# Where two loads of a written instruction order stand: in the middle of the opening, or behind its end

## The chip, the cores and the metric

One core of one Trainium2 chip runs the whole program. The metric is the device time of one execution in microseconds (us). Within 0.2% (2 us here) two versions of this kernel are called the same.

## The reference, cut to what matters

Rotary attention, then a mixture of experts, then a dense block, one after the other, float32 throughout:

```python
q, k, v: (4, 8, 576, 64)                      # 4 batches, 8 heads, 576 tokens
q_rot, k_rot = rotate(q), rotate(k)           # rotary embedding
scores = q_rot @ k_rot.T / sqrt(64)
attn = exp(scores - max); attn /= attn.sum() + 1e-9
x = (attn @ v) -> (2304, 512)                 # heads side by side
expert = argmax(x @ w_gate)                   # 8 experts, one per token
x = gate_w * (relu(x @ w1[expert]) @ w2[expert])
out = relu(x @ w_in)**2 @ w_out
```

## The kernel before, in words

The attention goes through 16 pairs of heads (P = 0 to 15). For each pair the work is cut into small steps, each named by a token: a letter, the pair, and a part. The ones that matter here:

- `L5` loads q and k of pair 5 (a tile `qk` of 1,280 KB, one DMA, line 244). `V5` loads v of pair 5 (tile `V`, 320 KB, line 248).
- `Q5..0` to `Q5..2` apply the rotary embedding on GpSimd in place in `qk` (lines 460 and 456). `H5` rounds the result to a high part on ScalarE (`XH`, line 261), `W5` takes the rest as a low part on GpSimd (`XL`, line 269).
- `Z5` stacks high and low parts by ten DMAs inside the chip (line 286), five for each head of the pair: `kZ` twice, `qZ` from `XH`, `QH`, and `qZ` from `XL` (160 KB each, `QH` 128).
- `S5.2` is one 128-row block of scores on TensorE (lines 310 and 312, tile `ps`); it reads `kZ`, `qZ` and `QH`. `M` takes its maximum on VectorE (line 320), `X` its exponential on ScalarE (line 327). The first block of a pair to run is number 2.
- `U` and `O` turn the exponentials on TensorE (line 345, tile `pp`) and copy them out (`eT`, `eL`). `A5.0` and `A5.1` multiply by `V` (line 372, tile `av`), `G` copies the result to `X` (line 375), `J` projects it, `F` divides by the sums; after pair 3 the routing of the first batch of tokens begins (tiles `rt_...`, on VectorE and GpSimd).

The order is written out by hand. `at(t, f)` puts a step on a heap with a planned time. The 298 tokens of the list `ORDER` get equal shares of the time 0 to `UNTIL` (90.30). Every other step gets the time 15.954 P plus a number from `OFF`. Steps are then given out in the order of these times, and each engine, SyncE (SP) with its DMA queue too, works through its own instructions in that order. Planned times are only a sort key; they are not times of the profile.

Buffers are in rings of a few: `qk` has two, `V` has two, `kZ` and `qZ` have four. A load into a buffer waits, on SP, until the last reader of what was there before is done; what follows on SP waits behind it. The reader counts wherever it stands in the order, also behind the load: `L7` is given out ahead of `W5`, whose tile it overwrites, and waits for it.

All loads and all stacking DMAs of the attention are issued by SP, in one queue.

Of the kernel before, what the change touches and what calls it, by code (L numbers as in the profile page):

```python
# [59 lines left out]
def shape_constants():  # L60
# [27 lines left out]
    for b in range(B):  # L88
        for c in range(4):
# [17 lines left out]
OFF = dict(pair=15.954, load=-26.0, v=8.0, rope=-11.279, hi=0.235, lo=1.675, z=4.815,  # L107
           S=[21.118, 20.135, 15.671, 27.85, 18.735, 24.184, 28.378, 24.712, 17.071],
           max=[21.846, 20.96, 16.399, 28.578, 19.463, 24.912, 29.183, 25.517, 18.084],
           exp=[22.666, 21.951, 17.479, 29.363, 20.248, 25.697, 30.078, 26.412, 18.869],  # L110
           un=[32.589, 32.153, 35.217, 38.036, 36.617, 23.748, 28.906, 37.6, 35.653, 34.253, 33.817],
           out=[33.418, 34.148, 36.917, 39.025, 37.411, 29.788, 32.958, 38.405, 36.294, 35.538, 34.643],
           av=[41.194, 44.969], x=[46.747, 47.789], pj=54.426, fin=58.03)
UNTIL = 90.30
# [15 lines left out]
def attention(tc, rope, ident, qk, v, w_gate, xd, on_batch, later, ahead):  # L130
# [18 lines left out]
    def at(t, f):  # L149
        heapq.heappush(sched, (round(t, 3), len(T["n"]), f))  # L150
        T["n"].append(0)
# [39 lines left out]
    def warm(n):  # L191
        nc.tensor.matmul(T["warm"][:, 0:n], T["hi", 0][:, 0, 0:128], T["hi", 0][:, 0, 0:n], start=True, stop=True)

    def do(token):
        k, a = token[0], [int(i) if i else None for i in token[1:].split(".")] if token[1:] else []
        if k in "SMXAG":
            dict(S=scores, M=smax, X=sexp, A=values, G=gathered)[k](*a)
        elif k in "UO":
            (turn if k == "U" else turned)(a[0], UNITS[a[1]])
        elif k in "RQ":  # L200
            rotate(a[0], a[1], nc.vector if k == "R" else nc.gpsimd, a[2])
        elif k in "Ww":
            low(a[0], a[1] if a[1:] else None, None if k == "W" else nc.vector)
        elif k == "E":
            for i in range(a[0]):
                warm(288)
        elif k in "bcd":
            dict(b=lambda: rotate(0, 1, nc.vector, cols=Z), c=lambda: direct_high(0, Z), d=lambda: direct_low(0, nc.vector, Z))[k]()
        else:
            dict(H=high, Z=stack_up, L=load, V=load_v, J=project, F=finish, K=gate_weights)[k](*a)  # L210

    def direct_high(P, cols):


        x, h = T["qk", P], T["hi", P]
        to = min(cols.stop, 512)
        for j in range(2):
            r = slice(64 * j, 64 * j + 64)
            nc.scalar.activation(QH[P][j][r, cols.start:to], x[r, 0, 1, cols.start:to], AF.Copy)
        if cols.stop > 512:  # L220
            nc.scalar.activation(h[:, 1, 512:640], x[:, 0, 1, 512:640], AF.Copy)

    def direct_low(P, eng, cols):
        x = T["qk", P]
        to = min(cols.stop, 512)
        for j in range(2):
            r = slice(64 * j, 64 * j + 64)
            minus(eng, T["qZ", 2 * P + j][r, cols.start:to], x[r, 0, 1, cols.start:to], QH[P][j][r, cols.start:to].bitcast(F32))
        if cols.stop > 512:
            minus(eng, T["lo", P][:, 1, 512:640], x[:, 0, 1, 512:640], T["hi", P][:, 1, 512:640].bitcast(F32))  # L230
# [19 lines left out]
    def rotate(P, n, eng, step=None, cols=slice(0, 640)):  # L250
        x, a = T["qk", P], slice(0, 2) if n is None else slice(n, n + 1)
        for i, (f, o, y) in enumerate(((times, 0, TB[:, 0, a, cols]), (times, 1, TB[:, 1, a, cols]), (plus, 0, x[:, 1, a, cols]))):
            if step in (None, i):
                f(eng, x[:, o, a, cols], x[:, o, a, cols], y)
# [8 lines left out]
    def low(P, n=None, eng=None):  # L263
        if ("lo", P) not in T:
            T["lo", P] = zp.tile([128, 2, 640], F32R, name="XL", tag="XL", bufs=2)
        a = slice(0, 2) if n is None else slice(n, n + 1)
        args = T["lo", P][:, a], T["qk", P][:, 0, a], T["hi", P][:, a].bitcast(F32)
        if eng is None:
            nc.gpsimd.tensor_sub(*args)
        else:  # L270
            minus(eng, *args)
# [139 lines left out]
    def route(P, t=None):  # L411
        t = OFF["pair"] * P + OFF["fin"] + .02 if t is None else t
        d = next(T["route", P], None)
        if d is not None:
            t += d
            at(t, lambda: route(P, t))
# [4 lines left out]
    for P in range(NPAIR):  # L421
        def on(o, token):
            if token not in ORDER:
                at(OFF["pair"] * P + o, lambda: do(token))

        if P > 2:
            on(OFF["load"], f"L{P}")
            for i in range(3):
                on(OFF["rope"] + 2.93 * i, f"Q{P}..{i}")
            for k, o in (("H", "hi"), ("W", "lo"), ("Z", "z")):  # L430
                on(OFF[o], f"{k}{P}")
        if P > 0:
            on(OFF["v"] + (1.8 if P == NPAIR - 1 else 0), f"V{P}")
        for k, o in (("S", "S"), ("M", "max"), ("X", "exp"), ("U", "un"), ("O", "out"), ("A", "av"), ("G", "x")):
            for u, t in enumerate(OFF[o]):
                on(t, f"{k}{P}.{u}")
        on(OFF["pj"], f"J{P}")
        on(OFF["fin"], f"F{P}")
        if P % 4 == 3 and P + 1 < NPAIR:
            at(OFF["pair"] * P + OFF["fin"] + .02, lambda P=P: route(P))  # L440
# [848 lines left out]
```

## Time and profile before

| | |
|---|---|
| median of 3 runs | 985.91 us (985.28 to 986.06) |
| the profiled execution | 987.28 us |
| its span, first to last instruction | 985.5 us |
| TensorE busy (PE) | 962.2 us, 98% of the span |
| VectorE (DVE), ScalarE (ACT), GpSimd (POOL) busy | 535.9, 422.8, 321.9 us |
| mean granted TensorE clock | 0.993 of full speed |
| attention, from the first instruction to the last `av` | about 300 us |

The profile lists instructions with the us from the span's start. In a timeline a row is the start, the time from the first start to the last end of the merged instructions, the engine, the line, the operation and its tiles, how many, and in brackets the idle time of the engine before the row and what ended it. `SPq` is SP issuing a DMA; a row of it ends when the issue is done, not when the data has landed.

### The profile page before, as it was taken

Reading aid. Unit: us, or ns where it says so; the run is one execution under the profiler, and the core shown is the slowest. Engines: PE = TensorE matmul, PEld = TensorE weight load, DVE = VectorE, ACT = ScalarE, POOL = GpSimd, SP = SyncE. Lnnn points to the kernel's source line nnn. Section 1 sums busy time; section 2 is a strip of 40 time slices with the busy share of each in tenths; the row PEclk is TensorE's granted clock in tenths of the full one; section 3 lists DMA queues with packets and bytes.
Section 4 is the critical chain, followed back from the end, with each engine's and each line's share of the span. In section 5 each row is a group of like instructions: output and inputs, shape, how many; then the busy total and the mean of one; then the engine's idle time right before and its main releaser. Section 6 shows DMA issues by size and latency. Waiting matters only on the chain. (4 is left out here: it accounts for less than half of the span.)

```text
span 985.5 us, 15576 instructions
## 1 busy us (share of the span) xinstructions
PE 962.2 (98%) x5589; PEld 826.9 (84%) x5589; DVE 535.9 (54%) x949; ACT 422.8 (43%) x840; POOL 321.9 (33%) x261
## 2 busy tenths in 40 slices
PE   8997999999999999999999999999999999999997
PEld 8785787878787888888888789999999999999996
DVE  7775677777876345575586469522322323222222
ACT  4665566666552123352465358522322222222222
POOL 2886487888475222233254300010010100100101
PEclk9999899999999999999999999999999999999999
DMA  6884786877542834455486523100000200100000
GB/s 219 242 249 128 200 227 185 231 206 196 169 121 92 274 124 130 130 172 183 138 283 223 183 96 135 33 33 1 32 33 1 65 1 22 43 1 1 33 1 33
DMA packets 46353, 119.83 MB, mean 122 GB/s; under 512 B 8240, under 2 KB 9776, under 8 KB 43952
## 3 DMA queue, kind: packets, MB, share of 16 engines
q1 hardware_dynamic: 40752, 101.58, 33.7%
q0 software_dynamic: 4960, 16.43, 4.9%
q8 instruction: 46, 0.75, 0.3%
q10 hardware_dynamic: 544, 0.66, 0.2%
q14 instruction: 51, 0.42, 0.1%
HBM read 79.93 MB, written 15.11 MB: 96 GB/s over the span
## 5 line engine op out<-in xcount | busy, mean ns | idle before, releaser
L1115 PE MATMUL o<-Wo,gs 128*128 128x512 f32 x864 | 214.7, 393 | 0.0
L1094 PE MATMUL h<-xs,Wi 128*128 128x384 f32 x1008 | 189.6, 336 | 0.0
L1115 PEld LDWEIGHTS o<-Wo,gs 128*128 128x128 f32 x864 | 159.9, 188 | 28.6 <-DVE gs L1105 0.3
L1094 PEld LDWEIGHTS h<-xs,Wi 128*128 128x128 f32 x1008 | 178.2, 188 | 6.6
L1103 DVE SCALAR_TENSOR_TENSOR g<-h,r 128x384 f32<-128x384 f32 x80 | 44.6, 558 | 190.5 <-ACT r L1099 190.5
L327 ACT ACTIVATE e<-ps,mx 128x576 f32<-128x576 f32 x144 | 106.3, 740 | 90.2 <-DVE mx L320 90.0
L1130 POOL DMA_INDIRECT out_dram<-os,at x18 | 17.8, 989 | 369.3 <-DVE os L1125 309.9
L320 DVE TENSOR_REDUCE mx<-ps 128x1 f32<-128x576 f32 x144 | 105.7, 752 | 57.6 <-PE ps L312 57.1
L1099 ACT ACTIVATE r<-h 128x384 f32<-128x384 f32 x96 | 47.1, 491 | 204.7 <-PE h L1094 204.7
L917 PE MATMUL p_y<-W,hh 128*128 128x512 f32 x504 | 124.5, 403 | 0.8 <-ACTq L929 0.8
L888 PE MATMUL p_h<-W,xs 128*128 128x512 f32 x480 | 114.8, 394 | 0.0
L917 PEld LDWEIGHTS p_y<-W,hh 128*128 128x128 f32 x504 | 94.3, 191 | 22.6 <-ACTq L929 1.1
L888 PEld LDWEIGHTS p_h<-W,xs 128*128 128x128 f32 x480 | 88.5, 188 | 18.4 <-DVEq L929 0.7
L345 PE MATMUL pp<-ident,e 128*128 128x128 f32 x640 | 86.2, 275 | 1.6 <-DVE eT L361 1.3
L1105 DVE TENSOR_TENSOR gs<-g,gs 128x384 fp32r<-128x384 f32 x96 | 53.7, 559 | 56.1 <-ACT gs L1104 56.1
L310 PE MATMUL ps<-kZ,qZ 128*128 128x288 f32 x300 | 72.0, 330 | 8.7 <-DMA qZ<-XL 7.4
L460 POOL TENSOR_TENSOR qk<-qk,TB 128x1280 f32<-128x1280 f32 (+1 forms) x28 | 79.2, 2844 | 2.1 <-DMA qk<-in_qk_dram 2.1
L345 PEld LDWEIGHTS pp<-ident,e 128*128 128x128 f32 x640 | 74.6, 142 | 5.3 <-issue 2.6
L1104 ACT ACTIVATE gs<-g 128x384 fp32r<-128x384 f32 x96 | 50.4, 526 | 50.5 <-DVE g L1103 50.0
L372 PE MATMUL av<-eT,V 128*64 128x288 f32 x512 | 69.1, 412 | 0.0
L361 DVE COPY eT<-pp 128x512 f32<-128x512 f32 x96 | 64.2, 683 | 7.3 <-PE pp L345 6.0
L310 PEld LDWEIGHTS ps<-kZ,qZ 128*128 128x128 f32 x300 | 45.9, 192 | 20.7 <-issue 11.8
(237 smaller groups left out, 1208.0 us busy)
## 6 DMA issues: line engine op xcount, KB each, us to landing
qk<-in_qk_dram SPq DMA_DIRECT2D x14, 1280.0 KB, 6.4
raw<-in_moe_w_dram SPq DMA_DIRECT2D x30, 512.0 KB, 4.6
kZ<-XH SPq DMA_DIRECT2D x60, 160.0 KB, 2.9
rawa<-in_moe_w_dram SPq DMA_DIRECT2D x18, 512.0 KB, 3.6
w<-in_moe_w_in_dram SPq DMA_DIRECT2D x8, 1024.0 KB, 5.2
w<-in_moe_w_out_dram SPq DMA_DIRECT2D x8, 1024.0 KB, 5.4
V<-in_v_dram SPq DMA_DIRECT2D x16, 320.0 KB, 4.1
qZ<-XH SPq DMA_DIRECT2D x30, 160.0 KB, 2.9
```

What stands on the lines that cost most here:

```text
L310: nc.tensor.matmul(t[:, u, 0:288], Q1[:, qs], K1[:, k0 + 288 * u:k0 + 288 * u + 288], start=i == 0, stop=False)
L320: nc.vector.tensor_reduce(small("mx", P, 9)[:, s:s + 1], T["S", P, s][:, :, 0:288], axis=AX.XY, op=ALU.max, negate=True)
L327: nc.scalar.activation(ed.rearrange("p (u n) -> p u n", u=2), T["S", P, s][:, :, 0:288], AF.Exp, bias=T["mx", P][:, s:s + 1], accum_out=SS ...
L345: nc.tensor.transpose(t[:, c * 128:c * 128 + 128], src, ident)
L361: nc.vector.tensor_copy(o, i)
L372: nc.tensor.matmul(t[64 * j:64 * j + 64], V[:, j, kc], eT[:, j, kc, cs] if kc < 4 else eL[:, cs], start=kc == 0, stop=kc == 4)
L460: v.tensor_tensor(out=out, in0=a, in1=b, op=ALU.mult)
L888: nc.tensor.matmul(t[u], s[:, a, k], W1[:, b, k, 512 * u:512 * u + 512], start=n == 0, stop=n == 11)
L917: nc.tensor.matmul(t, s[:, a, k], W2[:, b, k], start=n == 0, stop=n == 23)
L1094: nc.tensor.matmul(t, W[:, a, k, fs], s[:, c, k], start=n == 0, stop=n == 11)
L1105: nc.vector.tensor_sub(gs[:, 1], g, gs[:, 0].bitcast(F32))
L1115: nc.tensor.matmul(self.T["o", b][c], gs[:, a, 128 * c:128 * c + 128], W[:, w], start=(f == 0 and n == 0), stop=(f == 15 and n == 2))
```

## The change

Steps that are not in `ORDER` get a planned time of at least `UNTIL`.

```diff
     for P in range(NPAIR):
         def on(o, token):
             if token not in ORDER:
-                at(OFF["pair"] * P + o, lambda: do(token))
+                at(max(UNTIL, OFF["pair"] * P + o), lambda: do(token))
```

Of all steps outside `ORDER` two have a planned time below 90.30: `L7` with 15.954 x 7 - 26.0 = 85.68, and `V5` with 15.954 x 5 + 8.0 = 87.77. All other steps keep their place. Both now have the time 90.30, behind the last token of `ORDER` (`Z5`, 90.00) and ahead of the next step (`Q6..2`, 90.305); `V5` comes first, since pair 5 is listed ahead of pair 7. The order around the place, with the moved steps in capitals marked by stars:

```
before  ... O3.0 U3.9 *L7* S4.5 S4.7 O3.9 M4.5 M4.7 A3.0 X4.5 *V5* V4 Q6..0 W5 Q6..1 F2 X4.7 U4.5 Z5 Q6..2 S4.3 S4.6 ... A3.1 ...
after   ... O3.0 U3.9 S4.5 S4.7 O3.9 M4.5 M4.7 A3.0 X4.5 V4 Q6..0 W5 Q6..1 F2 X4.7 U4.5 Z5 *V5* *L7* Q6..2 S4.3 S4.6 ... A3.1 ...
```

On SP's queue this reads, before: `L6 L7 V5 V4 Z5 Z6 L8 V6`; after: `L6 V4 Z5 V5 L7 Z6 L8 V6`. The other queues hold the same instructions in the same order.

## Rows read from the trace of the kernel before

**Rows 1.** The page, part 1: busy us, share of the span, instructions of each engine.

```profile
PE 962.2 (98%) x5589; PEld 826.9 (84%) x5589; DVE 535.9 (54%) x949; ACT 422.8 (43%) x840; POOL 321.9 (33%) x261
```

**Rows 2.** Waits of PE, whole span: us in total, times, longest; the two longest.

```profile
PE ps L310 <- DMA qZ<-XL: 7.4, 1, 7.4
PE warm L480 <- POOL ss L168: 1.5, 1, 1.5
```

**Rows 3.** Timeline of PE: start, us, line, operation, count, idle before it.

```profile
76.03 0.66 PE L372 MATMUL av<-eL,V 128*64 128x288 f32 x4
...
92.21 0.66 PE L372 MATMUL av<-eL,V 128*64 128x288 f32 x4
100.27 0.82 PE L310 MATMUL ps<-kZ,qZ 128*128 128x288 f32 x2 [7.41 <-DMA qZ<-XL]
...
104.40 1.04 PE L345 MATMUL pp<-ident,e 128*128 128x128 f32 x8
...
118.53 0.53 PE L310 MATMUL ps<-kZ,qZ 128*128 128x288 f32 x2
...
120.83 1.04 PE L345 MATMUL pp<-ident,e 128*128 128x128 f32 x8
...
135.78 0.53 PE L310 MATMUL ps<-kZ,qZ 128*128 128x288 f32 x2
```

**Rows 4.** Windows: stretch, us, busy of each engine, granted clock, DMA share, GB/s.

```profile
92.80:100.20 7.40, 0.06 (x2) 0.00 (x0) 0.00 (x0) 1.59 (x2) 5.62 (x2) 0.81 0.82 199
100.20:104.40 4.20, 4.13 (x19) 4.14 (x20) 1.79 (x4) 1.32 (x3) 2.94 (x2) 0.52 0.95 225
```

**Rows 5.** Timeline of SP's queue around the place.

```profile
81.69 0.33 SPq L244 DMA_DIRECT2D qk<-in_qk_dram  x1
82.11 11.12 SPq L248 DMA_DIRECT2D V<-in_v_dram  x2
93.28 1.12 SPq L286 DMA_DIRECT2D kZ<-XH  x2
```

**Rows 6.** Waits of SP's queue from 60 to 93.3 us: total, times, longest.

```profile
SPq L248 <- PE av L372: 14.0, 2, 10.3
SPq L244 <- POOL XL L269: 11.1, 1, 11.1
```

**Rows 7.** Timelines of ACT and POOL, 77 to 104 us.

```profile
77.13 1.28 ACT L261 ACTIVATE XH<-qk 128x1280 fp32r<-128x1280 f32 x1
...
78.71 2.95 POOL L269 TENSOR_TENSOR XL<-qk,XH 128x1280 fp32r<-128x1280 f32 x1
...
94.58 2.88 POOL L269 TENSOR_TENSOR XL<-qk,XH 128x1280 fp32r<-128x1280 f32 x1 [7.04 <-ACT XH L261]
97.41 5.73 POOL L460 TENSOR_TENSOR qk<-qk,TB 128x1280 f32<-128x1280 f32 x2
```

**Rows 8.** Issue to landing, whole span, by tile: `qZ`, then `qk`, then `V`.

```profile
DMA to landing us min/median/max: 2.7/3.1/4.3
DMA to landing us min/median/max: 4.8/6.1/7.2
DMA to landing us min/median/max: 3.7/4.1/7.0
```

**Rows 9.** DMA of 93 to 101 us: packets, MB, mean rate (stacking DMAs and one `V`).

```profile
DMA packets 797, 1.64 MB, mean 205 GB/s; under 512 B 141, under 2 KB 141, under 8 KB 797
```

**Rows 10.** Timelines of POOL, DVE and SP, 115 to 126 us.

```profile
115.98 0.26 POOL L452 TENSOR_TENSOR rt_d<-lg,rt_mx 128x40 f32<-128x40 f32 x1 [12.83 <-DVE rt_mx L529]
...
116.97 2.93 POOL L456 TENSOR_TENSOR qk<-qk 128x1280 f32<-128x1280 f32 x1
...
117.74 0.18 DVE L540 TENSOR_REDUCE rt_mn<-rt_im 128x5 f32<-128x40 f32 x1
119.36 0.76 DVE L320 TENSOR_REDUCE mx<-ps 128x1 f32<-128x576 f32 x1 [1.44 <-PE ps L312]
...
124.85 0.81 SPq L286 DMA_DIRECT2D qZ<-XL  x1
```

## The prediction

> **What bounds the kernel now.** Begin with the page's busy times: TensorE works for 962.2 us of a span of 985.5 [rows 1], so at most 23.3 us of idle time can be won without taking work from it, and whatever the change brings must come from there. Next read the waits of TensorE over the whole span, longest first [rows 2]. The reader is to see that they are short but for one, 7.4 us, in which a block of scores waits for a stacking DMA (`qZ` from `XL`); the next longest is 1.5. Third, find that wait in TensorE's timeline [rows 3]: the last product with `V` before it, the end of `A3.1`, ends at 92.21 + 0.66 = 92.87, and the next matmul starts at 100.27. In the list of the order that matmul is `S5.2`, the first block of pair 5, and what it waits for is `Z5`. The question is why `Z5` was late. SP's timeline [rows 5] gives it: `L7` is issued at 81.69, then two loads of `V` (`V5`, `V4`) take from 82.11 to 93.23, then `Z5` begins at 93.28. SP's waits [rows 6] say what held them: `L7` waited 11.1 us for `XL` (`W5`), and one load of `V` 10.3 us for a product `av`. V5 and V4 fall on two buffers: one that pair 2 left when `A2.1` ended, at 76.03 + 0.66 = 76.69 [rows 3], the other held by pair 3 until `A3.1` ends at 92.87. `V5` came first and took the free one; `V4` waited for `A3.1`, and `Z5` stood behind it. Its inputs had long been there: `H5` ended at 77.13 + 1.28 = 78.41 and `W5` at 78.71 + 2.95 = 81.66 [rows 7]. Last the windows [rows 4]: in 100.2 to 104.4 the granted clock is 0.52, near the lower level of 1.2 GHz, after TensorE stood idle.
>
> **The change, part by part.** No instruction is added or removed; two loads move on SP's queue, past `V4` and the ten DMAs of `Z5`.
>
> *V4 ahead of V5.* `V4` now asks first and takes the buffer of pair 2, free at 76.69, and nothing waits in front of `Z5` but `H5` and `W5`. The first three kinds of its DMAs can be issued from 78.41 on, the `qZ` from `XL` from 81.66 on. With 0.6 us of issue (1.12 for two [rows 5]) and the longest landing of a `qZ`, 4.3 us [rows 8], the first head's operands are there at 81.66 + 0.6 + 4.3 = 86.6, which is 6.3 us before TensorE comes to `S5.2` at 92.87. Even if all five DMAs of that head were issued only from 81.66 on, 2.8 us of issue, it is 88.8. So the whole 7.41 us of waiting goes, and what ends last at `S5.2` is TensorE's own work. Its bounds: 7.41 if `Z5` comes as computed, 0 if `V4` still waits in front of it. I take 7.41.
>
> *The clock.* Behind the wait, TensorE's steps from 100.27 to 104.40 (`S5.2`, two turned blocks, `S5.8`) take 4.13 us [rows 3]. The same sequence of pair 6 stands in the same rows, from 118.53 to 120.83, at 2.30 us. Without the idle time the clock has no reason to fall (in no other wait of [rows 2] is TensorE idle so long), so 4.13 - 2.30 = 1.83 us goes too. Bounds: 0, if the clock falls all the same, and 2.07, half of 4.13, if every step halves. I take 1.83, which is a measured pair of equal steps.
>
> *V5 and L7 later.* `V5` now waits for `A3.1`, and `L7` stands behind it: `V5` is issued at about 93.0, `L7` at 93.35, 11.7 us later than the 81.69 of now. Behind them on SP is `Z6`, which cannot begin before `H6` is done: `W6` starts at 94.58, released by it [rows 7]. So the wait blocks nothing that was ready. `V5` is read by `A5.0`, which comes behind `S6.2` (due at 109.3, below); it has over 16 us for at most 7.0 [rows 8]. For `L7` the reader is `Q7..0` on GpSimd, which starts at 97.41 now, right behind `W6` [rows 7]. `L7` lands 4.8 to 7.2 us after its issue [rows 8]: 98.1 to 100.5, so GpSimd starts 0.7 to 3.1 us later. A harder bound: `V5` and `L7` together, 1.64 MB, at the 205 GB/s of the stretch in which the stacking DMAs run [rows 9], take 8.0 us: 101.3, 3.9 late. Does that reach TensorE? GpSimd's two steps of 5.73 us end at 103.8 to 106.2 (107.0 in the harder bound). Next in its order is the routing `rt_d`, at 115.98 now after 12.83 us of idle time [rows 10]; it waits for VectorE, whose work follows TensorE and moves up by the 9.24 us won, to 106.7. So the lateness is hidden by idle time, 0.5 us of which is left at the longest landing; in the harder bound `rt_d` is 0.3 late. That is covered too: VectorE's `rt_mn` at 117.74 reads `rt_im`, done by 117.01, and behind it VectorE is idle for 1.44 us, so some 2.1 us of lateness pass before a block of scores has to wait. I take 0, with 3.9 as the far end.
>
> The Trainium skill says the opposite of this part: its page "DMA: Bandwidth & Descriptors", section "Rules for kernel authors", advises issuing a DMA early and waiting on it late. By that rule `L7` should lose by its move. The rows here show both loads give up time in which nobody waits; by the rule, with the whole 3.1 us passed on to TensorE, the sum would be 6.14 instead of 9.24, and that is the second case below.
>
> *Z6, L8, V6.* `Z6` is issued from about 94.6, its `qZ` from `XL` when `W6` ends at 94.58 + 2.88 = 97.46. Behind the loads in the harder bound, with 0.79 MB for its first head (1.64 + 0.79) / 205 = 11.9 us from 93.3 on, that head is there at 105.2; `S6.2` is due at 118.53 - 9.24 = 109.3. `L8` needs `W6` and follows `Z6`, `V6` waits for `A4.1` as before. Nothing.
>
> *The rest.* From 104.40 on every later step waits for TensorE or for what TensorE has released, and the waits that are left are short [rows 2]. So the 9.24 us pass through to the end.
>
> **Sum.** 7.41 + 1.83 + 0 = 9.24 us. The profiled execution took 987.28 us, its span of 985.5 and 1.78 around it; it would take 978.04. It lies 1.37 above the median of the runs shown; from that median, 985.91 - 9.24 = 976.67.
>
> **The rivals.**
>
> *The late load is felt.* `L7` holds up GpSimd, this holds up `rt_im`, `rt_mn` and the maxima behind it on VectorE, and so the scores. For: at the longest landing only 0.5 us of GpSimd's idle time is left. Against: another 2.1 us on VectorE. If all of 0.7 to 3.9 us reaches TensorE the gain is 8.5 to 5.3, 977.4 to 980.6; at 3.1 us it is 979.8.
>
> *The change does not do what it says.* `V4` could be given the buffer of `V3` even when it comes first, and wait for `A3.1` ahead of `Z5` as now: 985.9. For: which buffer a tile gets is decided by the program that builds the kernel, and no row shows `V4` first. Against: in the rows the tile that came first, `V5`, took the one that was free first.
>
> *Slower: Z7 becomes what Z5 was.* `S7.2`, at 135.78 now [rows 3], is due at 126.5. Its chain from the landing of `L7`: 5.73 for two steps, 1.0 of routing, 8.7 from `Q7..2` (116.97) to the end of the issue of `qZ` (124.85 + 0.81), 4.3 of landing [rows 7, 8, 10], 19.7 in all. It begins to cost where `L7` lands after 106.8, 13.5 us after its issue. At 114.2 it takes back all: 7.4 of waiting and 1.83 of clock. At 116 it is 987.7. For: one queue carries all, and `L7` is now in the thick of it. Against: no `qk` took more than 7.2 us [rows 8].
>
> **Chances.** Forecast, 976.7, own range 975.5 to 978.0: 0.82. Late load felt, 978 to 980.6: 0.08. Some other limit keeps part of the stall, 980 to 983: 0.02. Without effect, 985.9: 0.05. Slower: 0.03. What a measurement can tell from no change is about 0.2%, 2.0 us. Faster by more is 0.82 + 0.08 + 0.02 = 0.92, within it 0.05, slower 0.03. The low end of the range is the sum with the clock's upper bound, 9.48, and half a us below the median as the runs scatter: 975.8, taken as 975.5. The high end reaches into the second case at 3.1 us, 979.8.
>
> **What the changed profile would show.** One load of `V` issued near 77 and `Z5` from about 78.5, done by 86; no wait of `S5.2` for `qZ`, its start at 92.9; granted clock 1.00 in 93 to 110; `L7` issued near 93.4 and `Q7..0` beginning 1 to 3 us after `W6` with a wait for `qk`; `rt_d` near 106.7 with little idle time before it; from `S6.2` (109.3) on the same distances as now. Wrong would be: a load of `V` still waiting for `A3.1` ahead of `Z5`; a wait of some us on TensorE between 105 and 127, for a maximum or for a `qZ` of `Z7`; or a gain at 110 us that is gone by 300.

## The result, and the profile after

The changed kernel takes 977.58 us (median of 6 runs, 976.01 to 978.55) against 985.98 (984.65 to 986.79) for the kernel before: ratio 0.9913, 95% interval 0.9900 to 0.9926, so 8.4 us less, with 7.3 to 9.9 by the interval. Run again beside the experiments, the ratio was 0.9904 (0.9888 to 0.9919). The forecast was 976.7 in a range of 975.5 to 979.8. The profiled execution took 977.97 us with a span of 976.2, 9.3 less than before.

The waits of TensorE over the span, where [rows 2] stood; the 7.4 us are gone and no other wait has grown:

```profile
PE warm L480 <- POOL ss L168: 1.5, 1, 1.5
PE pp L345 <- DVE eT L361: 1.2, 2, 1.0
```

TensorE's timeline, against [rows 3]. `S5.2` starts at 92.93, right behind `A3.1`; its sequence takes 2.30 us (92.93 to 95.23) as that of pair 6 (109.35 to 111.66) does:

```profile
92.34 0.66 PE L372 MATMUL av<-eL,V 128*64 128x288 f32 x4
92.93 0.53 PE L310 MATMUL ps<-kZ,qZ 128*128 128x288 f32 x2
...
95.23 1.04 PE L345 MATMUL pp<-ident,e 128*128 128x128 f32 x8
...
109.35 0.53 PE L310 MATMUL ps<-kZ,qZ 128*128 128x288 f32 x2
...
111.66 1.04 PE L345 MATMUL pp<-ident,e 128*128 128x128 f32 x8
```

The windows, against [rows 4]: full clock (third number from the end) and a TensorE that is never idle.

```profile
92.80:100.20 7.40, 7.40 (x62) 7.17 (x61) 6.00 (x11) 6.78 (x15) 2.93 (x1) 1.00 0.82 256
100.20:110.00 9.80, 9.80 (x76) 6.96 (x76) 7.22 (x18) 4.59 (x12) 8.75 (x6) 1.00 0.91 265
```

SP's queue, against [rows 5]: `V4` at 76.86, when `A2.1` is done; `Z5` from 78.57, its first `qZ` from `XL` at 81.58, the last at 85.21; then `V5`, which has waited for `A3.1`, and `L7`; `Z6` from 94.66.

```profile
76.86 0.33 SPq L248 DMA_DIRECT2D V<-in_v_dram  x1
78.57 1.12 SPq L286 DMA_DIRECT2D kZ<-XH  x2
...
81.58 0.46 SPq L286 DMA_DIRECT2D qZ<-XL  x1
...
85.21 0.60 SPq L286 DMA_DIRECT2D qZ<-XL  x1
93.04 0.33 SPq L248 DMA_DIRECT2D V<-in_v_dram  x1
93.41 0.43 SPq L244 DMA_DIRECT2D qk<-in_qk_dram  x1
94.66 1.11 SPq L286 DMA_DIRECT2D kZ<-XH  x2
```

GpSimd and VectorE, against [rows 7] and [rows 10]. GpSimd now waits 3.43 us for `L7`, and `rt_d` follows the two steps of `Q7` with no idle time where it had 12.83: it starts 9.14 us earlier, and the late load takes the rest. `rt_mn` still runs in its turn, and the 1.44 us of idle time behind it are untouched:

```profile
94.71 2.93 POOL L269 TENSOR_TENSOR XL<-qk,XH 128x1280 fp32r<-128x1280 f32 x1 [7.28 <-ACT XH L261]
101.07 5.80 POOL L460 TENSOR_TENSOR qk<-qk,TB 128x1280 f32<-128x1280 f32 x2 [3.43 <-DMA qk<-in_qk_dram]
106.84 0.24 POOL L452 TENSOR_TENSOR rt_d<-lg,rt_mx 128x40 f32<-128x40 f32 x1
...
108.56 0.18 DVE L540 TENSOR_REDUCE rt_mn<-rt_im 128x5 f32<-128x40 f32 x1
110.19 0.76 DVE L320 TENSOR_REDUCE mx<-ps 128x1 f32<-128x576 f32 x1 [1.44 <-PE ps L312]
```

The last projection of the attention is a good milestone, the same instruction in every kernel. First before, then after: 9.21 us earlier, so nothing was given back on the way.

```profile
302.03 1.49 PE L383 MATMUL pj<-R,X 128*128 128x144 f32 x10 [0.99 <-ACT X L375]
```

```profile
292.82 1.49 PE L383 MATMUL pj<-R,X 128*128 128x144 f32 x10 [0.99 <-ACT X L375]
```

### The profile page after: what moved, and what is told of

It is laid out like the page before. It is cut to its first block, busy times and chain, and to the rows that moved or that the text cites. A ratio compares the mean times of both kernels' runs of the same rounds, so it can differ in the third digit from the quotient of the medians.

```text
span 976.2 us, 15577 instructions
## 1 busy us (share of the span) xinstructions
PE 960.7 (98%) x5589; PEld 825.5 (85%) x5589; DVE 533.7 (55%) x949; ACT 423.0 (43%) x840; POOL 321.6 (33%) x261
## 5 line engine op out<-in xcount | busy, mean ns | idle before, releaser
L922 POOL DMA_INDIRECT yd<-yo,idx x21 | 21.3, 1013 | 120.6 <-DVE yo L921 89.8
```

## Experiments

### Which of the two loads it was

**Only L7 moved.**

```diff
-                at(OFF["pair"] * P + o, lambda: do(token))
+                at(max(UNTIL if token == "L7" else 0, OFF["pair"] * P + o), lambda: do(token))
```

> Only L7 goes behind the list, V5 stays in the middle. SP's queue: V5 V4 Z5 L7 Z6. Theory: V4 still waits for A3.1 ahead of Z5, Z5 is issued from 93.3, the wait of 7.4 us and the low clock stay: 986, no change. L7 is issued at about 100 and lands near 107, which the idle time of GpSimd up to 116 hides. Rival (L7 was the cost): most of the gain, 977 to 979.

Measured: 986.43 us, ratio 1.0002 (0.9992 to 1.0011). No change, as the theory had it. SP's two loads of `V` now take 16.51 us, to 92.98, with nothing but the wait for `A3.1` between them, `L7` follows `Z5` at 100.19, and `S5.2` waits 6.92 us (SP, then TensorE):

```profile
76.47 16.51 SPq L248 DMA_DIRECT2D V<-in_v_dram  x2
...
100.19 0.59 SPq L244 DMA_DIRECT2D qk<-in_qk_dram  x1
...
99.52 0.82 PE L310 MATMUL ps<-kZ,qZ 128*128 128x288 f32 x2 [6.92 <-DMA qZ<-XL]
```

**Only V5 moved.**

```diff
-                at(OFF["pair"] * P + o, lambda: do(token))
+                at(max(UNTIL if token == "V5" else 0, OFF["pair"] * P + o), lambda: do(token))
```

> Only V5 goes behind the list, L7 stays in the middle. SP's queue: L7 V4 Z5 V5 Z6. Theory (what cost time was any load of V that waits for A3.1 ahead of Z5): Z5 is issued from about 82.4, behind the wait of L7 for W5, and its first head has landed by some 90; S5.2 starts at 92.9 without a wait; the whole gain, 9.2 us, about 976.7. L7 lands early, so GpSimd starts Q7..0 at 97.4 with no wait for the load. Rival (L7 with its 1.28 MB ahead of Z5 was the cost, by its wait or by its transfer): most of the stall stays, 983 to 986.

Measured: 978.59 us, ratio 0.9918 (0.9905 to 0.9932). The theory holds in the main, but not in its "whole gain": the milestone stands at 295.00, 2.18 us behind the changed kernel's. Timelines of SP, then TensorE:

```profile
81.27 0.33 SPq L244 DMA_DIRECT2D qk<-in_qk_dram  x1
81.69 0.38 SPq L248 DMA_DIRECT2D V<-in_v_dram  x1
82.12 1.12 SPq L286 DMA_DIRECT2D kZ<-XH  x2
...
91.11 0.56 SPq L286 DMA_DIRECT2D qZ<-XL  x1
...
93.20 0.50 PE L310 MATMUL ps<-kZ,qZ 128*128 128x288 f32 x2 [0.52 <-ACT X L375]
...
96.88 0.50 PE L310 MATMUL ps<-kZ,qZ 128*128 128x288 f32 x2 [1.77 <-DMA qZ<-XL]
```

The first head of pair 5 is there almost in time: its last operand lands at 93.00, and `S5.2` waits 0.52 us. (The row names a step of ScalarE; in the changed kernel `S5.2` starts at 92.93 and that step at 93.05, so `S5.2` does not need it.) The second head is late: with `L7` and `V4` just ahead, `Z5` is issued over 9.55 us (82.12 to 91.67) where the changed kernel needs 7.24 (78.57 to 85.81). Its last operand is there just before 96.88, and `S5.8`, which reads both heads, waits 1.77. So `L7` ahead of `Z5` has a price of its own. It acts in two ways, which were not tried apart: its wait for `W5` holds back the first DMAs of `Z5`, and its 1,280 KB move ahead of them. An estimate says that the first alone does not make the wait: begun at 82.12, issued in 7.24 and landed in the 4.3 of [rows 8], the last operand would be there at 93.7, and `S5.8` was ready at 95.11. In whole executions this price is not resolved: the intervals of the two ratios overlap.

**V4 ahead of V5, both ahead of Z5.**

```diff
-... A3.0 X4.5 V4 Q6..0 W5 ...
+... A3.0 V4 X4.5 Q6..0 W5 ...
```

> The order of before, but V4 stands ahead of V5 (V4 and X4.5 change places in the list); both are ahead of Z5. Theory: V4 takes the free buffer and V5 waits for A3.1 in front of Z5: the wait of 7.4 us stays, 986. Rival (what mattered was that V4 came late, or that V4 and V5 came in the wrong order): the gain of the change, 977.

Measured: 986.42 us, ratio 0.9999 (0.9989 to 1.0008): no change. It is not the turn of `V4` and `V5` that mattered. Whichever comes second waits for `A3.1`, and in this kernel it does so in front of `Z5`; `S5.2` waits, and later `S5.8`, slow steps and all, waits a little for the second head:

```profile
99.68 0.82 PE L310 MATMUL ps<-kZ,qZ 128*128 128x288 f32 x2 [6.74 <-DMA qZ<-XL]
...
103.16 0.54 PE L310 MATMUL ps<-kZ,qZ 128*128 128x288 f32 x2 [0.16 <-DMA qZ<-XL]
```

### Whether the clock had a price of its own

The order of before, with work for TensorE in the time of the wait; the result of the 48 matmuls is overwritten.

```diff
             return
+        if (P, s) == (5, 2):
+            for i in range(48):
+                nc.tensor.matmul(t[:, i % 2, 0:288], T["lo", P][:, 0, 0:128], T["lo", P][:, 0, 0:288], start=True, stop=True)
```

> The order of before. In front of S5.2 stand 48 matmuls of 128x288 into its own output, whose result is overwritten; they run in the time in which TensorE waits for Z5 (about 6 of the 7.4 us). Theory: the wait itself stays (S5.2 starts near 100.3), but the granted clock stays at 1.00 and the steps behind it take 2.30 us and not 4.13: 1.8 us less than before, 984.1. Rival (the steps behind the wait are slow for another reason, contention with the stacking DMAs or their own operands): they take 4.1 us as before, 986.

Measured: 986.13 us, ratio 0.9998 (0.9988 to 1.0008). The 1.8 us did not come. TensorE's timeline, then two windows:

```profile
92.41 6.58 PE L309 MATMUL ps<-XL 128*128 128x288 f32 x48
99.56 0.49 PE L313 MATMUL ps<-kZ,qZ 128*128 128x288 f32 x2 [0.57 <-DMA qZ<-XL]
...
104.25 0.54 PE L313 MATMUL ps<-kZ,qZ 128*128 128x288 f32 x2 [2.79 <-DMA qZ<-XL]
...
92.40:99.00 6.60, 6.59 (x50) 6.35 (x48) 0.00 (x0) 1.59 (x2) 4.81 (x2) 1.00 0.75 190
99.00:105.00 6.00, 2.65 (x19) 2.45 (x20) 1.79 (x4) 1.32 (x3) 3.89 (x2) 1.00 0.89 214
```

The clock did stay at 1.00, the 2.4 GHz level, and the steps ran at their full pace. But then `S5.8` waits 2.79 us, for the second head of `Z5`, and the sequence ends at 104.89, where before it ended at 104.40 [rows 3]. In the kernel before, the slow steps had filled the time until the second head was there. Both theories missed that: the low clock was real, and behind it lay the next wait. The 2.79 us are more than this kernel shows for the one before, though. The trace records the landing of each DMA in sixteen parts. Here fifteen parts of that operand had landed at 102.90 and the last at 104.21; before, all had landed at 103.25. From there `S5.8` at full pace needs another 0.64 (104.25 to 104.89), so by this estimate the sequence of the kernel before could have ended at about 103.9, and keeping the clock up was worth at most some 0.5 us of the 1.83. The interval of the ratio rules out 1.8, but not 0.5.

### How late L7 may land

**L7 behind Z5, but ahead of V5.**

```diff
-                at(OFF["pair"] * P + o, lambda: do(token))
+                at(max(UNTIL - 0.1 * (token == "L7"), OFF["pair"] * P + o), lambda: do(token))
```

> As the change, but behind the list L7 stands ahead of V5, so that it does not wait for A3.1. SP's queue: V4 Z5 L7 V5 Z6. L7 is issued at about 86 and not 93.4, lands by 92. Theory (the lateness of L7 in the changed kernel is hidden by GpSimd's idle time): the time is that of the changed kernel within 0.2%, Q7..0 starts at 97.6 with no wait for the load, and rt_d gets idle time ahead of it again. Rival (the late load is felt): 1 to 3 us less than the changed kernel.

Measured: 977.55 us, ratio 0.9916 (0.9903 to 0.9930), beside 976.69 and 0.9904 (0.9888 to 0.9919) for the changed kernel run beside it:

> The changed kernel once more, beside the kernels below on one chip. By the sum of the prediction 9.2 us less than before (ratio 0.9906); by the median of its first runs 8.4 less (0.9915). In its trace one load of V and Z5 early, no wait of S5.2.

No difference that can be measured. GpSimd has its idle time in front of `rt_d` back, 3.40 us, and TensorE's milestone (292.75 here, 292.69 there) does not move:

```profile
97.56 5.81 POOL L460 TENSOR_TENSOR qk<-qk,TB 128x1280 f32<-128x1280 f32 x2
106.76 0.26 POOL L452 TENSOR_TENSOR rt_d<-lg,rt_mx 128x40 f32<-128x40 f32 x1 [3.40 <-DVE rt_mx L529]
```

**L7 done twice, and three times**, in the changed kernel.

```diff
-            nc.sync.dma_start(out=t, in_=src)
+            for _ in range(2 if P == 7 else 1): nc.sync.dma_start(out=t, in_=src)     # 3 in the second kernel
```

> As the change, but the load L7 is done twice, into the same place, one behind the other. Theory (2.1 us of lateness of rt_d pass, what is beyond reaches TensorE): L7 lands some 6 us later, near 107, GpSimd's two steps end near 113 and rt_d is 6 us late, so 3 to 5 us come back: 980.5 to 983. Rival (a load of qk is never felt this far ahead of its scores): 977.5, as the changed kernel.

Measured: 982.14 us, ratio 0.9961 (0.9946 to 0.9976), 5.45 us over the changed kernel. GpSimd waits 9.01 us for the load, `rt_d` starts at 112.20 (106.71 in the changed kernel run beside it), VectorE waits 4.80 in front of `rt_mn`, and TensorE 1.01 and 2.96 for what VectorE and ScalarE bring late. `Z6`, which stands behind the second load, adds 0.22 and 0.95. At the milestone this kernel is 7.64 us behind (300.33 against 292.69): 5.14 are these four waits, and the other 2.5 go with the clock, which falls in the last of them (granted 0.50 in 118 to 122.7, 0.79 over 110 to 126, where the changed kernel has 1.00). The whole executions differ by less than the milestones; the last section tells what differs behind it. Timelines of GpSimd, VectorE, TensorE, then a window:

```profile
106.48 5.77 POOL L460 TENSOR_TENSOR qk<-qk,TB 128x1280 f32<-128x1280 f32 x2 [9.01 <-DMA qk<-in_qk_dram]
112.20 0.27 POOL L452 TENSOR_TENSOR rt_d<-lg,rt_mx 128x40 f32<-128x40 f32 x1
...
113.27 0.20 DVE L540 TENSOR_REDUCE rt_mn<-rt_im 128x5 f32<-128x40 f32 x1 [4.80 <-POOL rt_im L460]
...
109.47 0.50 PE L310 MATMUL ps<-kZ,qZ 128*128 128x288 f32 x2 [0.22 <-DMA qZ<-XL]
...
112.33 0.51 PE L310 MATMUL ps<-kZ,qZ 128*128 128x288 f32 x2 [0.95 <-DMA qZ<-XL]
...
114.54 0.66 PE L345 MATMUL pp<-ident,e 128*128 128x128 f32 x4 [1.01 <-DVE eL L361]
...
118.16 0.85 PE L310 MATMUL ps<-kZ,qZ 128*128 128x288 f32 x2 [2.96 <-ACT e L327]
...
110.00:126.00 16.00, 11.08 (x71) 10.38 (x70) 7.31 (x13) 7.16 (x15) 15.34 (x15) 0.79 0.90 268
```

> As the change, but the load L7 is done three times, into the same place. Theory: L7 lands near 113, and Z6 behind it in SP's queue is late as well: S6.2, due at 109.3, waits some 5 us for qZ, and rt_d is late by over 10. This is the slower case of the prediction: about all of the gain gone, 983 to 989. Rival (lateness is hidden by idle time): below 981.

Measured: 987.21 us, ratio 1.0016 (1.0005 to 1.0027): the whole gain is gone. SP is held for 11.34 us by the three loads, `S6.2` waits 4.87 us for `Z6`, which stands behind them, and the lateness of `rt_mn` costs another 2.50; here, too, the granted clock is low behind the first wait (0.50 in 114.4 to 119.5):

```profile
93.54 11.34 SPq L244 DMA_DIRECT2D qk<-in_qk_dram  x3
...
114.42 0.82 PE L310 MATMUL ps<-kZ,qZ 128*128 128x288 f32 x2 [4.87 <-DMA qZ<-XL]
...
122.75 0.53 PE L310 MATMUL ps<-kZ,qZ 128*128 128x288 f32 x2 [2.50 <-ACT e L327]
```

## Why the prediction was right, point by point

- *V4 ahead of V5 frees Z5; 7.41 us.* Shown. `V4` took the buffer of pair 2, `Z5` was issued from 78.57 (forecast 78.5), and the wait is gone. The runs with one load moved, and with `V4` and `V5` exchanged, show what the step is about: a load that waits for a buffer, in front of DMAs that are ready and needed. The prediction put the whole of it on the loads of `V`. That was too simple: moving `V5` alone brings the milestone to 295.00, 7.03 us earlier, and the last 2.18 come only with `L7` behind `Z5` as well. The prediction also timed the first head alone, and not the second, which `S5.8` needs. In the changed kernel the second was in time as well (issued by 85.81, and `S5.8` runs without a wait), so the term came out, but the prediction had not worked that out.
- *The clock, 1.83 us.* The size is right: the sequence went from 4.13 to 2.30. The reason was half of it. Keeping the clock up with `Z5` late brings nothing that can be measured, and by the estimate above at most some 0.5 us, since the second head is the next to be late. The clock and the second head both go back to the late `Z5`, so the term could stand in the sum; as a price of the clock alone it would have been wrong.
- *V5 and L7 later, at no cost.* Right, and closer than it looked. `L7` was read 7.66 us after its issue began (93.41 to 101.07), beyond the 7.2 of [rows 8] and near the harder bound of 101.3 [rows 9]: the DMAs of `Z6` were issued from 94.66 on, while it was on its way (with `L7` ahead of `V5`, and no such DMAs beside it, it landed 5.6 us after its issue). Of the 12.83 us of idle time in front of `rt_d` none is left here, and 0.41 in the second profile. That it costs nothing is shown by the kernel with `L7` ahead of `V5`. The 2.1 us of lateness that the prediction let pass are about right for the wait: with the doubled load `rt_d` is 5.49 us late, which would by that leave 3.4, and TensorE's waits of this chain are 3.97. The price of the lower clock behind such a wait, some 2.5 us there, was missing from the prediction's second case.
- *Z6, L8, V6: nothing.* Right; `S6.2` starts at 109.35 with no wait (forecast 109.3).
- *The rest passes through.* Right: 9.21 us at the milestone, 9.3 in the span, 9.24 forecast. The medians' 8.4 in the first runs and the ratio 0.9904 of the second lie about it, within their intervals.
- *The rivals.* That `V4` would wait all the same is ruled out by its row at 76.86. The late load is not felt here, but is real: doubled, it takes 5.45 us, with what it does to `Z6` behind it. The slower case needed a landing some 13 us later than it came; with the load done three times it happened, though mostly by another way than priced: `Z6` and `S6.2` were late before `Z7` and `S7.2` could be. The advice that the prediction takes from the Trainium skill (page "DMA: Bandwidth & Descriptors", section "Rules for kernel authors"), to issue a DMA early, did not decide here: `L7` was issued 11.7 us later and nothing was lost, while ten DMAs that were needed sooner no longer stood behind a load that could not start.
- *The range.* Its low end is 985.91 - 9.48 - 0.5 = 975.9 by the prediction's own terms, not 975.8; this changes nothing.

## What to carry to other kernels

In a queue that works in order, a load that must wait for its buffer holds back everything behind it, however ready: put the transfers that are needed next ahead of it, and look at what each load waits for, not only at when it will be needed. When one wait is removed, look for the next one behind it (here the second head behind the first, hidden by slow steps) before its time is put down to another cause. Idle time on an engine off the path is a budget. Of GpSimd's 12.83 us the move-up of everything else took 9.1 and the late load the rest; with the load 5.49 us later still, TensorE lost more than that at the milestone, 7.64, since `Z6` came late too and the clock fell.

## What the runs showed of the hardware that was not expected

The granted clock also drops in some profiles and not in others at a place that no kernel here changed, the start of the expert stage. The six executions of the changed kernel, too, have mean granted clocks from 0.996 to 1.000. Windows of 310 to 325 us of the kernel before, and of the one whose TensorE was kept busy during the wait:

```profile
310.00:325.00 15.00, 14.64 (x70) 12.21 (x71) 11.47 (x49) 3.35 (x7) 6.12 (x7) 0.89 0.11 36
```

```profile
310.00:325.00 15.00, 14.27 (x75) 11.97 (x76) 11.20 (x47) 3.35 (x7) 6.11 (x7) 1.00 0.12 36
```

From the milestone to the end of the span the first takes 985.5 - 302.03 = 683.5 us, the second 984.4 - 302.43 = 682.0; the changed kernel, with a granted clock of 0.66 in 310 to 315, takes 976.2 - 292.82 = 683.4, and the one with only `V5` moved 976.7 - 295.00 = 681.7. That is 1.4 to 1.8 us from one profile to another over code that is the same in all four, and with single profiles it hides most of the 2.18 us between those last two: their spans differ by 0.5. In the same way the doubled load (681.4 from there on, without the drop) and the changed kernel beside it (683.1, with it) differ by 7.64 at the milestone and by 5.9 in the span. Of the ten traces here the four with the drop take 683.0 to 683.5 from the milestone on, and five without it 681.4 to 681.9; the kernel with `L7` ahead of `V5` has no drop and takes 683.0 all the same, so the clock is not all of it. What sets it was not tried.

The last of a DMA's sixteen parts can be late by itself. `S5.8` waits for such a part in two kernels: in the one kept busy it landed 1.31 us behind the other fifteen, in the one with only `V5` moved 1.17 (95.57 and 96.74). In the traces of these two, and of the kernels before and after, the last part begins to lag where a 16 KB transfer of the instruction queue runs: at 101.46 in the one kept busy, at 86.24 with only `V5` moved, at 83.84 in the changed kernel, where nobody waited. Whether the one causes the other was not tried.
